# Store order, bias-gradient sums and square placement in a one-core training step of a gated FFT filter and a squared-ReLU MLP

## Chip, core and metric

The kernel runs on one core of one Trainium2 chip. The metric is the device time of the core in microseconds, the median over several executions. A profile is one further execution, recorded by the hardware profiler; its times are measured from the span's start.

## The reference

The program computes a forward pass and all gradients of it, in bfloat16, for a sequence of 2048 rows of 1024 columns and a hidden width of 3584:

```python
g = sigmoid((x * gate_w).sum(-1))            # one gate per row
a = irfft2(rfft2(x) * (w_r + 1j * w_i))      # spectral filter over both axes
h = relu(x @ w1 + b1) ** 2                   # MLP, squared relu
b = h @ w2 + b2
out = g * a + (1 - g) * b
# outputs: out, and the gradients of x, w_r, w_i, w1, b1, w2, b2, gate_w for a given grad_out
```

The gradient of b2 is the sum over the 2048 rows of `db = (1 - g) * grad_out`, one number for each of the 1024 columns.

## The kernel before

The kernel is written in a tile framework: the program text gives each instruction a priority, and a scheduler puts each engine's instructions into a fixed order when the kernel is built. An instruction whose inputs are early can be put far ahead of its place in the text. `after(ins, earlier)` makes `ins` wait for `earlier`; with `NoSync` it only fixes the order of two instructions on the same engine. `later["last"]` is the eviction (`dhT`) that was written last in the text. `ld` issues a DMA from SP, `st` from POOL (GpSimd).

The work runs in stages. The change touches the first one, `mlp_in`, beside which the side work (`first_stage_of_x`, `first_stage_of_grad`, `fft_mid`) is spread in small steps, one and a half (later 1.15) to each step of the main work.

**The first passes.** Four passes `k` over 512 rows each load rows of x (`xsrc`) and of grad_out (`dbn`), compute the gate, scale `dbn` by it (`gate`, L664), and turn both into columns on TensorE (`turn_x`, `turn_grad`, results `xT` and `dbT`). For the first two column pairs of W1, `forth` computes the hidden layer and `back_` the gradient `dh` (matmuls `pd`, L742, evicted on VectorE to `dhT`, L746). Each pass stores its four gated row tiles to `db_scr` (L1620, and L1631 for the last), one MB each, and adds them up in float32 (`sum_of_db`, L1590). After the passes, `column_sums` and `sums_out` (L972 to L984) reduce that accumulator over the partitions: a transpose on VectorE, a reduction, a small matmul with `sel`, a copy and a store.

**The units.** For the other columns of W1, a `Unit` (fp, sp) computes a 256 by 1024 block of the hidden layer from seven products in place of eight. The sums of quarters of x (`x_sums`, L817, four for each half of the rows) lie in the memory of `dbn`, which they may overwrite only once its rows have been stored to `db_scr`; the sums of quarters of W1 (`w_sums`, L831) lie in `Sw`, or for odd fp in the last rows of `dbn`. Each unit's products p1, p5, p6, p7, p4, p3, p2 (of the next unit) are interleaved with four `back_` of the unit before, and the unit yields four times. The accumulator X is copied by ScalarE (`cu`, `u2`, L845) before TensorE may add the next product to it. `rest` makes the relu: for one of the four blocks ScalarE reads PSUM (L856); for the other three VectorE first adds the copied part and the bias (L858), and ScalarE then makes one relu over both blocks of c = 0 (L862) and one over the third (L860). The squares (L727) follow directly, and the store of `h2T` follows p3. W1's next columns are loaded by SP at the beginning of a unit with sp = 0, into one of two buffers (L764).

**The spectral side work.** `first_stage_of_x` does, for each row tile i: load a source (L635), `folds` on VectorE and ScalarE (L258 to L271), `row_stage` (matmuls `pk`, L279), `first_columns` (matmuls `pu`, evictions `w`, `u`, a store to `z_scr` in three DMAs, L228). `fft_mid` begins with `edges`, which gathers from `z_scr` the values at three frequencies in twelve small DMAs of 2-byte elements (L338 to L340): eight of them 64 partitions by 16 elements, four of 64 elements. Then it loads its filters (`ab`, `wn`) and inputs (`z`).

Of the kernel before, what the change touches and what calls it, by code (L numbers as in the profile page):

```python
# [10 lines left out]
P = 128  # L11
# [128 lines left out]
def kernel(  # L140
# [179 lines left out]
    def fft_mid(filler):  # L320
# [7 lines left out]
        def edges():  # L328

            ed = fb.tile([P, NM, 2, 4], FDT, name="ed", tag="ed")  # L330
            low = fb.tile([P, NM, 4], FDT, name="low", tag="low")
            mid = fb.tile([P, 4], FDT, name="mid", tag="mid")
            nc.vector.memset(ed[lanes[1], 0], 0.0)
            col = z_scr[:].rearrange("c r x h t l -> r c h l x t")[:, :, 0, 0]
            for x in range(2):
                for t in range(2):
                    e = 2 * x + t
                    ld(out=ed[lanes[0], :, 0, e], in_=col[:, 0:NM, x, t])  # L338
                    ld(out=low[lanes[1], :, e], in_=col[:, NM:, 1 - x, t])
                    ld(out=mid[lanes[0], e : e + 1], in_=col[:, NM, 1 - x, t : t + 1])  # L340
            return ed, low, mid
# [324 lines left out]
    def first_stage_of_x():  # L666
        f, ft = {0: folds(f1, xs[0], later["last"])}, {}
        for i in range(NT + 1):
            if i + 3 < NT:
                xs[i + 3] = source(i + 3, x_perm, later["last"])  # L670
            if i < NT:
                ft[i] = row_stage(f1, f[i], kf[:], later["last"])
                yield
            if i > 0:
                first_columns(f1, cf, 0, i - 1, ft[i - 1], later["last"])
            if i + 1 < NT:
                f[i + 1] = folds(f1, xs[i + 1], later["last"])
            yield
# [23 lines left out]
    def mlp_in():  # L702
# [23 lines left out]
        def squared(rT, h2T):  # L726
            nc.scalar.activation(h2T, rT, ACT.Square)  # L727
# [106 lines left out]
        class Unit:  # L834
# [8 lines left out]
            def copied(self, tag):  # L843
                t_ = wb.tile([P, SW], FP32, name=tag, tag=tag, bufs=1)
                nc.scalar.copy(out=t_[:], in_=self.X[:])  # L845
                return t_

            def rest(self, c, j, acc, add=None):
# [4 lines left out]
                whole = self.rT[c]  # L853
                rT = rTs[self.fp, s, c] = whole[:, j, :]
                if add is None:
                    nc.scalar.activation(rT, acc[:], ACT.Relu, bias=bias)  # L856
                else:
                    STT(out=rT, in0=acc[:], scalar=bias, in1=add[:], op0=ALU.add, op1=ALU.add)  # L858
                    if c:
                        nc.scalar.activation(rT, rT, ACT.Relu)  # L860
                if (c, j) == (0, 1):
                    nc.scalar.activation(whole[:], whole[:], ACT.Relu)  # L862
                if (c, j) in ((0, 1), (1, 0)):
                    squared(whole[:], h2_of(self.fp, self.sp)[:, c])
# [26 lines left out]
            def p3(self):  # L891
                self.chain(self.V, S_[self.fp][4], x_quads(self.sp)[1][1], False)
                self.rest(0, 1, self.V, self.u2)
                store(h2T_scr, h2.pop((self.fp, self.sp)), self.fp, self.sp)

        later["x_sums"] = x_sums
        load_w1(0)
# [23 lines left out]
        for n, u in enumerate(units_):  # L921
# [3 lines left out]
            u.p1()  # L925
            back_(*waiting[0])
# [3 lines left out]
            u.p6()  # L930
            back_(*waiting[1])
            next(more_sums, None)
            if u.sp == 1 and u.fp < LAST:
                w_sums(u.fp + 1)
# [7 lines left out]
            if pr == 0 and u.sp == 0:  # L942
                later["blocks"] = later["last"]
                if 0 < fg < FG - 1:
                    load_w2(fg + 1, later["last"])
            u.p4()
# [7 lines left out]
        again(slice(8, NT))  # L954
        more = [(LAST, s, c) for c in range(2) for s in range(2)]
# [628 lines left out]
    acc = f1.tile([P, D], FP32, name="gb2", tag="gb2")  # L1584

    def sum_of_db(n):
        if n == 1:
            V(out=acc[:], in0=dbn[:, 0, :], in1=dbn[:, 1, :], op=ALU.add)
        elif n:
            V(out=acc[:], in0=acc[:], in1=dbn[:, n, :], op=ALU.add)  # L1590

    sums_of_x = None
    for k in range(NT // 4):
# [13 lines left out]
        sum_of_db(i), sum_of_db(i + 1)  # L1607
# [5 lines left out]
        sum_of_db(i + 2)  # L1613
# [3 lines left out]
        sum_of_db(i + 3)  # L1617
        next(units)
        if k:
            st(out=db_scr[:, i - 4 : i, :], in_=dbn[:, i - 4 : i, :])  # L1620
# [9 lines left out]
        if k == 3:  # L1630
            st(out=db_scr[:, i : NT, :], in_=dbn[:, i : NT, :])  # L1631
# [6 lines left out]
    sums_out(f1, fps, "ps2", column_sums(f1, acc, "tr_"), out_7)  # L1638
# [84 lines left out]
```

## Time and profile before

| | |
|---|---|
| Median of 3 runs | 1269.1 us (1268.01 to 1273.19) |
| The profiled execution's own time | 1265.81 us |
| Its span, first to last instruction | 1264.0 us |
| Mean granted TensorE clock | 0.996 of full speed |
| TensorE matmuls busy | 1213.3 us, 96% of the span |
| VectorE busy | 849.8 us, 67% |
| ScalarE busy | 553.2 us, 44% |
| GpSimd busy | 373.1 us, 30% |
| DMA moved | 242.75 MB, mean 192 GB/s |

In the profile's lines PE is TensorE, PEld its weight loads, DVE VectorE, ACT ScalarE, POOL GpSimd and SP SyncE; L12 is line 12 of the kernel. A row of instructions names the output and the inputs of an operation by the program's names. In a timeline the first number is the start in us, the second the duration, and a bracket at the end is the time that the engine was idle before, with what ended that wait. The waits are listed as: engine, line and output that waited, what it waited for, us in total, number of times, the longest. In the page's second part each digit is the busy share, in tenths, of one of forty equal slices of the span. A few per cent of the matmul records are missing in a trace.

### The profile page before, as it was taken

What the parts mean: (1) busy time and instruction counts of PE and PEld (TensorE: products, weight loads), DVE (VectorE), ACT (ScalarE), POOL (GpSimd) and SP (SyncE); (2) the same over time, 40 slices, a digit from 0 to 9 for tenths busy, and PEclk for the clock granted to TensorE, in tenths of its full rate; (3) what the DMA queues carried; (4) which work ended last, traced back from release to release, by engine and by line L of the source; (5) the groups of instructions that cost most, each with busy time, mean ns of one, the idle gap of its engine ahead of it and who ended that gap; (6) DMA issues with size and microseconds to landing.
All of it is one profiled execution on the core that took longest, in us unless ns stands there. A gap on an engine that the chain in (4) does not pass through costs nothing.

```text
span 1264.0 us, 18724 instructions
## 1 busy us (share of the span) xinstructions
PE 1213.3 (96%) x6527; PEld 587.9 (47%) x6648; DVE 849.8 (67%) x1940; ACT 553.2 (44%) x1006; POOL 373.1 (30%) x620
## 2 busy tenths in 40 slices
PE   7998999997999999999999999999999999999998
PEld 4554545543444444444444445555445444444443
DVE  3987668744788779677766552443876765896573
ACT  3566768863777753444445544555222210011110
POOL 0123424421333332323335545654122010000000
PEclk9999999999999999999999999999999999999999
DMA  9868465765465989889969969985799987666520
GB/s 290 288 179 182 135 203 175 189 167 151 155 184 166 229 245 188 175 192 223 248 164 284 195 155 250 218 224 166 182 242 210 212 190 190 180 185 184 169 85 34
DMA packets 329593, 242.75 MB, mean 192 GB/s; under 512 B 197868, under 2 KB 284042, under 8 KB 328730
## 3 DMA queue, kind: packets, MB, share of 16 engines
q1 hardware_dynamic: 297968, 146.43, 51.8%
q0 software_dynamic: 31328, 95.07, 23.5%
q8 instruction: 52, 0.85, 0.3%
q14 instruction: 43, 0.35, 0.1%
q10 hardware_dynamic: 202, 0.04, 0.0%
HBM read 111.43 MB, written 86.00 MB: 156 GB/s over the span
## 4 chain that ended last, share of the span: by engine, by line
PE 71%; DVE 15%; ACT 4%; DMA 4%; issue 4%; SPq 2%; POOL 0%; DVEq 0%; ACTq 0%
PE pw L1206 15%; PE acc L1289 13%; PE pd L742 8%; PE xX L1399 7%; PE pX L1078 6%; PE ph L841 5%; PE pV L1078 4%; PE xV L1399 3%; ACT x L419 2%; PE xZ L1399 2%; SPq L181 2%; DVE dhT L746 1%; PE pui L312 1%; DMA w1g<-in_B_w_dram 1%; PE pki L565 1%
## 5 line engine op out<-in xcount | busy, mean ns | idle before, releaser
L742 PE MATMUL pd<-dbT,w2T 128*128 128x512 bf16 x859 | 209.5, 383 | 10.0 <-DVE dhT L746 6.8
L742 PEld LDWEIGHTS <-w2T 128*128 128x128 bf16 x896 | 87.3, 99 | 111.3 <-issue 15.1
L1206 PEld LDWEIGHTS <-res 128*128 128x128 bf16 x896 | 86.6, 98 | 99.6
L1206 PE MATMUL pw<-odd,res 128*128 128x512 bf16 x498 | 112.5, 379 | 0.7
L746 DVE SCALAR_TENSOR_TENSOR dhT<-pd,rT 128x512 bf16<-128x512 f32 x112 | 76.7, 685 | 44.4 <-PE pd L742 38.3
L1357 ACT ACTIVATE g<-gatew_bc,dsc 128x1024 f32<-128x1024 bf16 x16 | 18.3, 1148 | 177.3 <-DVE dT L1408 98.3
L1206 PE MATMUL pw<-even,res 128*128 128x512 bf16 x374 | 84.0, 379 | 0.5
L419 ACT CAST x<-px 64x512 f16<-64x512 f32 x128 | 74.2, 579 | 19.7 <-PE px L416 18.4
L228 POOL DMA_DIRECT2D z_scr<-u x96 | 58.7, 617 | 80.8 <-ACT u L296 40.8
L228 POOL DMA_DIRECT2D r<-y_scr x96 | 58.5, 613 | 72.8 <-issue 41.5
L1399 PEld LDWEIGHTS <-dS 128*128 128x128 f16 x448 | 43.8, 98 | 53.3 <-DVE dS L1386 0.5
L1208 ACT CAST wo<-pw 128x512 bf16<-128x512 f32 x56 | 32.6, 584 | 81.8 <-PE pw L1206 81.8
L1289 PEld LDWEIGHTS <-even 128*128 128x128 bf16 x448 | 43.4, 98 | 50.3
L1289 PEld LDWEIGHTS <-odd 128*128 128x128 bf16 x448 | 43.2, 98 | 49.3
L1290 DVE SCALAR_TENSOR_TENSOR ot<-acc,omg,af 128x512 bf16<-128x512 f32 x32 | 24.0, 749 | 56.2 <-PE acc L1289 56.1
L727 ACT ACTIVATE h2T<-rT 128x1024 bf16<-128x1024 bf16 x56 | 59.1, 1057 | 0.7
L1289 PE MATMUL acc<-w2high,even 128*128 128x512 bf16 x249 | 57.1, 379 | 0.4
L1289 PE MATMUL acc<-w2high,odd 128*128 128x512 bf16 x249 | 57.0, 379 | 0.4
L1078 PEld LDWEIGHTS <-S 128*128 128x128 f16 x336 | 32.4, 98 | 45.6 <-DVE S L1065 7.4
L456 POOL DMA_DIRECT2D y_scr<-pc x64 | 36.1, 564 | 52.4 <-DVE pc L453 46.0
L1399 PE MATMUL xX<-dT,dS 128*128 128x512 f16 x224 | 51.0, 379 | 0.1
L394 POOL COPY w<-wn 128x512 bf16<-128x512 bf16 x32 | 23.8, 744 | 90.1 <-DVE tt L427 79.1
(262 smaller groups left out, 2496.1 us busy)
## 6 DMA issues: line engine op xcount, KB each, us to landing
h2T_scr<-h2T POOLq DMA_DIRECT2D x28, 512.0 KB, 4.4
dhT_scr<-dhT POOLq DMA_DIRECT2D x28, 512.0 KB, 4.8
z<-z_scr SPq DMA_DIRECT2D x64, 128.0 KB, 3.2
y_scr<-pc POOLq DMA_DIRECT2D x64, 128.0 KB, 4.1
ax_scr<-yo POOLq DMA_DIRECT2D x32, 256.0 KB, 4.5
out_dram<-wo POOLq DMA_DIRECT2D x56, 128.0 KB, 5.0
even<-h2T_scr SPq DMA_DIRECT2D x8, 896.0 KB, 8.7
odd<-h2T_scr SPq DMA_DIRECT2D x8, 896.0 KB, 7.3
```

Source lines behind the costliest of these rows:

```text
L228: issue(out=a, in_=b) if stored else issue(out=b, in_=a)
L419: nc.scalar.copy(out=x[lanes[n], c, :, 0:HW], in_=px[lanes[c], n])
L456: st(out=y_scr[:][c, :, :, h].rearrange("r x t l -> (r x) t l"), in_=pc[:, n])
L727: nc.scalar.activation(h2T, rT, ACT.Square)
L742: mm(pd[:], lhsT=w_[:, ec, fc % FGC * P : (fc % FGC + 1) * P], rhs=dbT[:, ec, ss], start=(ec == 0), stop=(ec == DC - 1),)
L746: return STT(out=dhT, in0=pd[:], scalar=2.0, in1=rT, op0=ALU.mult, op1=ALU.mult, accum_out=gb1part[:, fc, sb : sb + 1],)
L841: mm(acc[:], lhsT=lhs[:, t, :], rhs=rhs[:, t, :], start=start and t == 0, stop=t == KH - 1, skip_group_check=True)
L1078: self.mm = mm(acc[:], lhsT=lhs[:, t, c_], rhs=rhs[:, t, :], start=start and t == 0, stop=t == KH - 1, skip_group_check=True,)
L1206: mm(pw[:], lhsT=xr[:, t, d_ * P : (d_ + 1) * P], rhs=cur[:, t, :], start=(t == 0), stop=(t == NT - 1))
L1208: nc.scalar.copy(out=wo[:], in_=pw[:])
L1289: turn["PE"] = mm(acc[:], lhsT=cur[:, fc, t2 * P : (t2 + 1) * P], rhs=w2[fc // NT][:, fc % NT, cs], start=(fc == 0), stop=(fc == FC - 1))
L1399: mm(acc[:], lhsT=lhs[:, fc, :], rhs=rhs[:, fc, :], start=start and fc == 0, stop=fc == KH - 1, skip_group_check=True,)
```

## The change

Six edits, all in or beside the first stage:

1. The twelve edge loads of `edges` are issued by POOL (`st`) and not by SP (`ld`).
2. In `first_stage_of_x` the folds of tile i+1 are written ahead of the yield that separates `row_stage` of tile i from `first_columns` of tile i-1, and no longer behind `first_columns`.
3. In a `Unit`, both blocks of c = 0 get a relu of their own (512 columns each), and the squares leave `rest`: they are made in the next unit, the first ordered behind that unit's copy in p1, the second, followed by the store of `h2T`, behind its copy in p6.
4. The gradient of b2 is no longer accumulated from `dbn`. Sixteen reductions on VectorE sum halves of the rows of `dbT` (128 partitions by 1024 elements each), one in each of the units 1 to 16; in unit 17 the two halves are added, turned by one transpose on TensorE, copied and stored. They carry no order of their own.
5. `w_sums` moves from behind the second `back_` of a unit to behind the fourth and behind the sum of item 4.
6. The stores to `db_scr` wait for `later["last"]`. Pass 1 has none any more; pass 2 stores the rows of the first two passes, pass 3 those of the third, and the last follow as before. At these places `later["last"]` is the third eviction of pass 2's `back_`, and then the fourth.

```diff
@@ -335,9 +335,9 @@
             for x in range(2):
                 for t in range(2):
                     e = 2 * x + t
-                    ld(out=ed[lanes[0], :, 0, e], in_=col[:, 0:NM, x, t])
-                    ld(out=low[lanes[1], :, e], in_=col[:, NM:, 1 - x, t])
-                    ld(out=mid[lanes[0], e : e + 1], in_=col[:, NM, 1 - x, t : t + 1])
+                    st(out=ed[lanes[0], :, 0, e], in_=col[:, 0:NM, x, t])
+                    st(out=low[lanes[1], :, e], in_=col[:, NM:, 1 - x, t])
+                    st(out=mid[lanes[0], e : e + 1], in_=col[:, NM, 1 - x, t : t + 1])
             return ed, low, mid
 
         def some_am(h):
@@ -670,11 +670,11 @@
                 xs[i + 3] = source(i + 3, x_perm, later["last"])
             if i < NT:
                 ft[i] = row_stage(f1, f[i], kf[:], later["last"])
+                if i + 1 < NT:
+                    f[i + 1] = folds(f1, xs[i + 1], later["last"])
                 yield
             if i > 0:
                 first_columns(f1, cf, 0, i - 1, ft[i - 1], later["last"])
-            if i + 1 < NT:
-                f[i + 1] = folds(f1, xs[i + 1], later["last"])
             yield
 
     def first_stage_of_grad():
@@ -723,8 +723,8 @@
         def d_bank(name):
             return banks[-1].tile([P, SW], FP32, name=name, tag="ph", bufs=2)
 
-        def squared(rT, h2T):
-            nc.scalar.activation(h2T, rT, ACT.Square)
+        def squared(rT, h2T, behind_=None):
+            after(nc.scalar.activation(h2T, rT, ACT.Square), behind_, mybir.DependencyClass.NoSync)
 
         def new_rT():
             return wb.tile([P, 2, SW], BF16, name="rT", tag="rT", bufs=3)
@@ -842,7 +842,7 @@
 
             def copied(self, tag):
                 t_ = wb.tile([P, SW], FP32, name=tag, tag=tag, bufs=1)
-                nc.scalar.copy(out=t_[:], in_=self.X[:])
+                self.copy = nc.scalar.copy(out=t_[:], in_=self.X[:])
                 return t_
 
             def rest(self, c, j, acc, add=None):
@@ -850,18 +850,17 @@
                 bias = b1col[:, fc : fc + 1]
                 if c not in self.rT:
                     self.rT[c] = new_rT()
-                whole = self.rT[c]
-                rT = rTs[self.fp, s, c] = whole[:, j, :]
+                rT = rTs[self.fp, s, c] = self.rT[c][:, j, :]
                 if add is None:
                     nc.scalar.activation(rT, acc[:], ACT.Relu, bias=bias)
                 else:
                     STT(out=rT, in0=acc[:], scalar=bias, in1=add[:], op0=ALU.add, op1=ALU.add)
-                    if c:
-                        nc.scalar.activation(rT, rT, ACT.Relu)
-                if (c, j) == (0, 1):
-                    nc.scalar.activation(whole[:], whole[:], ACT.Relu)
-                if (c, j) in ((0, 1), (1, 0)):
-                    squared(whole[:], h2_of(self.fp, self.sp)[:, c])
+                    nc.scalar.activation(rT, rT, ACT.Relu)
+
+            def square(self, c, behind_=None):
+                squared(self.rT[c][:], h2_of(self.fp, self.sp)[:, c], behind_)
+                if c:
+                    store(h2T_scr, h2.pop((self.fp, self.sp)), self.fp, self.sp)
 
             def p2(self):
                 self.Z = d_bank("pZ")
@@ -891,9 +890,23 @@
             def p3(self):
                 self.chain(self.V, S_[self.fp][4], x_quads(self.sp)[1][1], False)
                 self.rest(0, 1, self.V, self.u2)
-                store(h2T_scr, h2.pop((self.fp, self.sp)), self.fp, self.sp)
 
         later["x_sums"] = x_sums
+        gb2 = wb.tile([P, DC, 2], FP32, name="gb2", tag="gb2")
+
+        def sum_of_db(n):
+            ec, h = divmod(n, 2)
+            nc.vector.reduce_sum(out=gb2[:, ec, h : h + 1], in_=dbT[:, ec, h * S // 2 : (h + 1) * S // 2], axis=mybir.AxisListType.X)
+
+        def grad_of_b2():
+            whole = wb.tile([P, DC], BF16, name="gb2b", tag="gb2b")
+            V(out=whole[:], in0=gb2[:, :, 0], in1=gb2[:, :, 1], op=ALU.add)
+            pb = fps.tile([DC, P], BF16, name="pb2", tag="ps2", bufs=2)
+            nc.tensor.transpose(pb[:], whole[:], identb[:])
+            row = wb.tile([DC, P], BF16, name="gb2r", tag="gb2r")
+            nc.vector.tensor_copy(out=row[:], in_=pb[:])
+            st(out=out_7.rearrange("(c p) -> c p", p=P), in_=row[:])
+
         load_w1(0)
         yield
         load_w1(1)
@@ -923,15 +936,17 @@
             if u.sp == 0 and u.fp < LAST:
                 load_w1(u.fp + 1)
             u.p1()
+            if n:
+                units_[n - 1].square(0, u.copy)
             back_(*waiting[0])
             u.p5()
             yield
             next(more_sums, None)
             u.p6()
+            if n:
+                units_[n - 1].square(1, u.copy)
             back_(*waiting[1])
             next(more_sums, None)
-            if u.sp == 1 and u.fp < LAST:
-                w_sums(u.fp + 1)
             yield
             u.p7()
             back_(*waiting[2])
@@ -943,6 +958,12 @@
                 later["blocks"] = later["last"]
                 if 0 < fg < FG - 1:
                     load_w2(fg + 1, later["last"])
+            if 0 < n <= 2 * DC:
+                sum_of_db(n - 1)
+            elif n == 2 * DC + 1:
+                grad_of_b2()
+            if u.sp == 1 and u.fp < LAST:
+                w_sums(u.fp + 1)
             u.p4()
             u.p3()
             if n + 1 < len(units_):
@@ -952,6 +973,7 @@
             if (u.fp, u.sp) == (LAST - 1, 0):
                 again(slice(0, 8))
         again(slice(8, NT))
+        units_[-1].square(0), units_[-1].square(1)
         more = [(LAST, s, c) for c in range(2) for s in range(2)]
         for this, that in zip(more, waiting):
             forth(*this, True)
@@ -1581,15 +1603,6 @@
     rows_of_x(1)
     st(out=cf[:], in_=cten["cf"].ap())
     stage = None
-    acc = f1.tile([P, D], FP32, name="gb2", tag="gb2")
-
-    def sum_of_db(n):
-        if n == 1:
-            V(out=acc[:], in0=dbn[:, 0, :], in1=dbn[:, 1, :], op=ALU.add)
-        elif n:
-            V(out=acc[:], in0=acc[:], in1=dbn[:, n, :], op=ALU.add)
-
-    sums_of_x = None
     for k in range(NT // 4):
         i = 4 * k
         if k + 1 < NT // 4:
@@ -1604,20 +1617,18 @@
         next(units)
         turn_grad(i + 3) if k else (turn_grad(i + 2), turn_grad(i + 3))
         next(units)
-        sum_of_db(i), sum_of_db(i + 1)
         if stage:
             next(stage)
         next(units)
         if k + 1 < NT // 4:
             turn_x(i + 4), turn_x(i + 5)
-        sum_of_db(i + 2)
         next(units)
         if k + 1 < NT // 4:
             turn_x(i + 6), turn_x(i + 7)
-        sum_of_db(i + 3)
         next(units)
-        if k:
-            st(out=db_scr[:, i - 4 : i, :], in_=dbn[:, i - 4 : i, :])
+        if k > 1:
+            for n in (i - 8, i - 4) if k == 2 else (i - 4,):
+                after(st(out=db_scr[:, n : n + 4, :], in_=dbn[:, n : n + 4, :]), later["last"])
         if k + 1 < NT // 4:
             gate(4 * (k + 1))
         if k + 2 < NT // 4:
@@ -1628,14 +1639,13 @@
             stage = first_stage_of_x()
         next(stage)
         if k == 3:
-            st(out=db_scr[:, i : NT, :], in_=dbn[:, i : NT, :])
+            after(st(out=db_scr[:, i:NT, :], in_=dbn[:, i:NT, :]), later["last"])
             for _ in later["x_sums"](0):
                 pass
         next(units)
         next(stage)
     V(out=gpg[:], in0=gcol[:], in1=omg[:], op=ALU.mult)
     later["more_banks"]()
-    sums_out(f1, fps, "ps2", column_sums(f1, acc, "tr_"), out_7)
 
     def aside():
         yield from stage
```

## The prediction

> **What bounds the kernel now.** I read the page first, then the table of windows of 20 us, then TensorE's waits, then the timeline around each long wait.
>
> ```profile
> PE   7998999997999999999999999999999999999998
> DVE  3987668744788779677766552443876765896573
> ACT  3566768863777753444445544555222210011110
> DMA  9868465765465989889969969985799987666520
> ```
>
> Each digit is 31.6 us. TensorE is full in the second half, so only its gaps can be won. The windows say where they lie: of 480 us up to 480, TensorE is idle for 33 us; from 560 to 1240 no window has over 0.9 us of it, except one of 1.6. The change touches only the first part. TensorE's waits from 87 to 470 us (total, times, longest):
>
> ```profile
> PE pd L742 <- DVE dhT L746: 6.6, 3, 5.9
> PE pk L279 <- ACT f L271: 6.4, 7, 2.8
> PE ph L841 <- ACT cu L845: 5.1, 6, 1.5
> ```
>
> One wait of 5.93 us is half of the first row and more. The timeline shows its chain (start, duration, engine, line; in brackets the idle time before it):
>
> ```profile
> 266.87 0.69 SPq L338 DMA_DIRECT2D ed<-z_scr  x1
> ...
> 277.54 0.92 SPq L340 DMA_DIRECT2D mid<-z_scr  x1
> ...
> 287.73 0.52 SPq L764 DMA_DIRECT2D w1g<-in_B_w_dram  x1
> ...
> 293.37 0.76 DVE L831 TENSOR_TENSOR dbn<-w1g 128x512 f16<-128x512 bf16 x2 [9.13 <-DMA w1g<-in_B_w_dram]
> 294.04 0.68 DVE L746 SCALAR_TENSOR_TENSOR dhT<-pd,rT 128x512 bf16<-128x512 f32 x1
> ...
> 294.79 4.93 PE L742 MATMUL pd<-dbT,w2T 128*128 128x512 bf16 x16 [5.93 <-DVE dhT L746]
> ```
>
> Twelve edge loads hold SP from 266.87 to 278.46. Behind them come filters and inputs, and the load of W1 only at 287.73. The sums of W1's quarters (L831) stand at the head of VectorE's queue for 9.13 us, the eviction dhT stands behind them, and TensorE stops. The 16 matmuls after it take 4.93 us where undisturbed rows of 16 take 3.45: the granted clock in the window 280 to 300 is 0.91. A smaller stretch of the same kind:
>
> ```profile
> 118.60 0.62 PE L279 MATMUL pk<-kf,f 128*128 128x128 f16 x8 [1.77 <-ACT f L271]
> ...
> 122.96 0.42 DVE L258 TENSOR_TENSOR uv<-src 128x512 f16<-128x512 bf16 x1 [3.32 <-DMA src<-in_A_x_dram]
> ...
> 126.23 0.62 PE L279 MATMUL pk<-kf,f 128*128 128x128 f16 x8 [2.82 <-ACT f L271]
> ```
>
> and the start of the kernel:
>
> ```profile
> 15.57 0.54 POOL L1620 DMA_DIRECT2D db_scr<-dbn  x1 [12.04 <-DVE dbn L664]
> ...
> 24.45 1.89 PE L642 MATMUL pt<-identb,xsrc 128*128 128x128 bf16 x16 [2.38 <-DMA xsrc<-in_A_x_dram]
> ...
> 31.31 1.23 DVE L817 TENSOR_TENSOR dbn<-xT 128x2048 f16<-128x2048 bf16 x1 [1.64 <-ACT xT L643]
> ```
>
> The last line matters for the order: L817 is written at the end of the fourth pass and runs at 31 us. What is not tied runs where its engine is free, far from where it is written.
>
> **The change, part by part.** Sums are against the profiled execution (span 1264.0, its own time 1265.8 us); the median of the three runs is 3.3 us above that.
>
> *Edge loads from SP to POOL, sums of W1 later.* SP loses 11.6 us of issuing. In the unit of 315 us, the W1 load is issued at 315.43, 0.03 us after the matmuls of p4 that free its buffer (314.37 plus 1.03). In the unit of 280 those matmuls end at 280.23 (279.20 plus 1.03), so the load could start 7.5 us before 287.73. The sums then start near 285.9, VectorE has waited 1.7 us instead of 9.13, and the wait of 5.93 and the slow matmuls' 1.48 go: -7.4 us. If ab, wn and z still keep SP, nothing is won: 0. I take -7.4, since these loads (278.50 to 287.63) need 9.1 us of SP and can begin at 267. W1's sums also move two turns back in the text; they ran before their place already, so I count nothing. POOL gets twelve issues. No row there has 1024 pieces of 2 bytes; 64 pieces take 0.54 us (gw), 256 take 0.73 (h2T), so I estimate 0.54 to 1.6 each, 6 to 15 us of POOL. Behind them on POOL stands dhT's store, at 267.44 now; its buffer is wanted again near 284, and a store lands 4.8 us after issue. Up to 12 us it costs nothing, at 15 it gives back 3.
>
> The Trainium skill, "DMA: Bandwidth & Descriptors", section "Issuing engines are not separate DMA queues", says that another issuing engine saves only the sequencer's time, usually small beside the transfer. Here the row shows 11.6 us of issue against 3.3 to 5.1 us of landing each; by that rule this part would be about 0, and the sum -1.6 instead of -9.0.
>
> *Stores of gated rows.* Now one MB each at 15.57, 35.03, 56.73 and 77.27. Tied behind the third and fourth evictions of the third pass (74.70 and 76.89), all four leave POOL between 75.4 and 79. Early, DMA is at 0.96 and 0.99 of its share; the wait of 2.38 us for xsrc, with a clock of 0.72 in the 5 us behind it (1.4 us), is worth up to 3.8 us. The load itself is issued late, behind SP's transposes (until 18.61), so I take -1.0. Later, three MB more meet a stretch at 1.0 (80 to 120). A store lands 5.0 to 10.1 us after issue, so the first two are down at 82 to 90. L817 overwrites those rows and must now wait; TensorE wants its result at 90.17, and on VectorE everything behind L817 waits too. Between 0 and +10 (8 of waiting and 1.5 of slow clock); I take +2.2, near the short end, since 65 to 75 has DMA idle at 0.01 to 0.26 and queues are short then.
>
> *Gradient of b2.* Removed: 15 adds of 1.21, the transpose of 1.23, the reduction of 1.21 and small pieces: 21 us of VectorE before 92, where DVE is the releaser of waits of 0.70 and 0.49 at 55 to 58 and in the chain of 1.21 at 60.63. L817 leaves that stretch too. Of these 2.4 I take -1.2, since early halves of the new sums can fill the holes. Added: 16 reductions of 128x1024, for which the nearest row is L975, 1.21: 19.4 us, and a last step of a few tenths. They are tied to nothing. VectorE is at 12 to 17 of 20 us from 120 to 260 and at 16 to 19 from 340 to 420. Bounds: 0 if all fill holes, +19.4 if each stands before an urgent eviction. VectorE waits 21 us for pd before its evictions between 80 and 300, so holes exist: I take an eighth, +2.4.
>
> *Folds a turn earlier.* VectorE and ScalarE get folds before first_columns, where both had stood 2 us behind z_scr stores (116.8). The wait of 1.77 at 118.60 should go, or most of it; the 2.82 at 126.23 hangs on src, issued at 115.06 behind SP's transposes, and stays. But uv then reaches the head of VectorE's queue a turn earlier and blocks evictions while src is missing: up to +4. From -6.3 (1.77, 2.82, and 1.7 of slow matmuls behind them: 1.77 us for four, 2.67 for eight, against 1.03 and 1.73) to +4; I take -1.5.
>
> *Squares behind copies.* Two squares of 1.06 leave the places ahead of the next unit's copies; the wide relu of 1.05 becomes two of 0.63, 0.2 us more per unit, hidden while ScalarE is at 6 to 17 of 20 (4.8 us over 23 units if it were not). TensorE's waits on cu and u sum to 5.6 us, all after 310 but the first, and L419's casts, which stay, stand in the same queue. Between -5.6 and +1; I take -2.5. The store of h2T comes half a unit later; its second buffer covers that (without it, a square would wait 4.4 us for the landing).
>
> Sum: -7.4 - 1.0 + 2.2 - 1.2 + 2.4 - 1.5 - 2.5 = -9.0, and 1269.1 - 9.0 = 1260 us.
>
> **Rivals.** (a) VectorE becomes the bound: the untied row sums, at 1.21 each, stand before evictions in units 1 to 16. For it: the wait at 284 shows that one held instruction there stops TensorE, and 340 to 420 has 1 to 4 us of holes in 20. Against: the 21 us of waiting for pd. If all of it counts, 19.4 - 2.4 more: 1277. It turns the sign once 0.7 us of each sum lies on the path (11.4 over 16). (b) The W1 load is not earlier, or POOL's edges hold dhT's store as long: without the 7.4, 1267.5, no change. For it: fourteen other loads stand between. (c) The four stores meet and L817 holds VectorE until 90: +8 on the forecast, 1268. Against: DMA is idle just before. (d) All the waits go, none comes: -7.4 - 3.8 - 2.4 - 6.3 - 5.6 is -26; half of what lies beyond my terms gives 1252.
>
> **How the numbers follow.** Forecast 0.44, (a) 0.20, (b) 0.16, (c) 0.10, (d) 0.10. A measurement of this kernel can tell 0.5% (6.3 us) from no change. Faster: (d) and most of the forecast, 0.52; same: (b), (c) and a little of the forecast, 0.28; slower: (a), 0.20. The range takes in (d) at its lower side with some more, and (a): 1249 to 1277. The faster cases alone run from 1249 to 1263.
>
> **What would show it.** Right: no VectorE wait above 3 us on w1g near 285, the clock at 1.00 in that window; the twelve ed, low, mid issues on POOL within 15 us; db_scr's four stores between 75 and 80; row sums in holes, with TensorE's waits on dhT under 2 us in all; waits on cu halved. Wrong: W1's load still issued over 5 us after p4, a VectorE wait on db_scr at L817, a new pk wait on src, or row sums in front of evictions from 100 to 360. A gain above 20 us or a loss would mean that the scheduler's order changed in ways that I don't see from here.

## The result and the profile after

The changed kernel takes 1254.84 us (median of 4 runs, 1248.74 to 1258.46) against 1269.13 before (4 runs, 1268.01 to 1273.19): a ratio of 0.9877, 95% interval 0.9831 to 0.9923. That is 14.3 us less; the forecast was 9.1 less. The profiled execution of after took 1253.29 us, its span is 1251.5 (12.5 less than before), and its mean granted clock is 0.997.

The page's second part, of after (each digit 31.3 us):

```profile
PE   8988999999999999999999999999999999999998
...
DVE  3869767746888868777866642444876765896573
ACT  4656867855777652444445544655222210011110
...
DMA  9587575786464979899979969995999787666530
```

Three of PE's digits moved: the first from 7 to 8, the third (63 to 94 us) from 9 to 8, and the tenth (284 to 316 us), which holds the W1 stall near 290 us, from 7 to 9; all others are the same. So this stall is gone, and something new stands in the third slice. The table of TensorE's waits from 87 to 470 us says what (total, times, longest):

```profile
PE ph L841 <- ACT u L845: 10.9, 6, 7.5
PE pu L312 <- ACT ft L283: 2.4, 3, 1.2
PE pk L279 <- ACT f L271: 2.0, 3, 0.8
...
PE pd L742 <- DVE dhT L746: 0.9, 2, 0.5
...
PE ph L841 <- ACT cu L845: 0.8, 2, 0.5
```

The dhT row fell from 6.6 to 0.9, pk from 6.4 to 2.0, cu from 5.1 to 0.8. In their place stands one row of 10.9 us for u, 7.5 of it in one wait, and a small one for ft. Without that one wait, u and cu together are 4.2 us, where before has 5.6.

The timeline round the W1 load, after (start, duration, engine, line; idle time before it in brackets):

```profile
264.19 0.84 POOL L338 DMA_DIRECT2D ed<-z_scr  x1
...
273.70 0.54 POOL L340 DMA_DIRECT2D mid<-z_scr  x1 [1.34 <-DMA ed<-z_scr]
...
274.99 0.73 POOL L773 DMA_DIRECT2D dhT_scr<-dhT  x1 [0.74 <-DMA low<-z_scr]
...
279.83 0.39 SPq L764 DMA_DIRECT2D w1g<-in_B_w_dram  x1
...
285.15 0.76 DVE L831 TENSOR_TENSOR dbn<-w1g 128x512 f16<-128x512 bf16 x2 [1.30 <-DMA w1g<-in_B_w_dram]
...
285.83 0.68 DVE L746 SCALAR_TENSOR_TENSOR dhT<-pd,rT 128x512 bf16<-128x512 f32 x1
```

The last `mid` and the first `dhT` store are POOL's now. SP issues the W1 load at 279.83 and no longer at 287.73. VectorE waits 1.30 us for it and not 9.13, dhT follows 0.68 us after the first pair of sums, and TensorE does not wait. In the window from 280 to 300 the clock is 1.00 (0.91 before).

The new wait, in the timeline round 95 us of after:

```profile
71.50 11.01 SPq L181 DMA_TRANSPOSE w2T<-in_B_w_dram  x2
...
82.57 2.44 SPq L635 DMA_DIRECT2D src<-in_A_x_dram  x2
...
85.11 8.17 SPq L764 DMA_DIRECT2D w1g<-in_B_w_dram  x2
...
93.37 9.85 SPq L635 DMA_DIRECT2D src<-in_A_x_dram  x2
95.41 0.42 DVE L258 TENSOR_TENSOR uv<-src 128x512 f16<-128x512 bf16 x1 [7.99 <-DMA src<-in_A_x_dram]
...
96.20 0.20 ACT L265 COPY f<-uv 128x2 f16<-128x2 f16 x1 [6.70 <-DVE uv L259]
96.30 0.58 ACT L845 COPY u<-ph 128x512 f32<-128x512 f32 x1
96.93 1.87 PE L841 MATMUL ph<-dbn,Sw 128*128 128x512 f16 x4 [7.49 <-ACT u L845]
```

It reads from the top. SP is held 11.01 us by the transposed loads of W2, then issues two sources (L635) from 82.57, then is held 8.17 by the loads of W1. The four stores of gated rows, four MB, were issued between 68 and 79. The DMA engines' share is 1.07 from 70 to 75 us and 1.08 from 75 to 80, where before has 0.26 and 0.55; from 80 to 100 it is 1.03, where before has 1.01 too. So from 80 us on they are about as full as in before; what differs is that they have been full for some ten us longer, with the stores and the transposes ahead of the sources. These are slow to land. From the list of DMA issues between 82 and 90 us of after (KB each, median us from issue to landing; the sources take 6.0 in before, where they are issued at 85.06, later than here):

```profile
w1g<-in_B_w_dram SPq DMA_DIRECT2D x2, 512.0 KB, 13.6
...
src<-in_A_x_dram SPq DMA_DIRECT2D x2, 256.0 KB, 12.8
```

The folds were moved a turn earlier, so `uv` is at the head of VectorE's queue and waits 7.99 us. ScalarE's small copy of `f` (L265) waits 6.70 for uv. Behind it in ScalarE's order stands the copy `u`, and TensorE waits 7.49 for that. From 96.9 to 101.0 the granted clock is 0.50, so those 4.1 us do the work of 2.05: the stall costs some 9.5 us in all. (The Trainium skill, "TensorE: Matmul & The Clock Gate", section "What's actually happening", says that a TensorE idle for a window of about 3.4 us falls to half its clock and comes back after about as long a busy stretch; the 0.50 over 4.1 us agrees. In before the clock is 0.72 from 25 to 30 us, behind a wait of 2.38 us, so a shorter one costs too.)

The four stores of gated rows and the sixteen row sums of after, from POOL's timeline and from the answer for one line:

```profile
68.53 1.39 POOL L1631 DMA_DIRECT2D db_scr<-dbn  x2 [3.97 <-DVE dhT L746]
...
75.66 0.58 POOL L1631 DMA_DIRECT2D db_scr<-dbn  x1
...
78.42 0.58 POOL L1642 DMA_DIRECT2D db_scr<-dbn  x1
```

```profile
L899 DVE TENSOR_REDUCE gb<-dbT x16: 1210/1214/1218, 39.0 to 133.3; 128x1 f32<-128x1024 bf16 x16
its engine sat idle before it (us, times) until:
who waited for it (us, times):
```

The stores leave POOL between 68.5 and 79; 75 to 80 was expected, and the third pass now ends some 6 us sooner. The sums ran from 39 to 133 us, VectorE was not held idle before any, and nobody waited for one. They are written in units 1 to 16, but are tied to nothing and took the first holes.

**One table for all kernels.** The 112 evictions `dhT` (L746) come in the same order of the text in every kernel. So the time between the starts of the 12th, 16th, 24th, 56th, 64th and 112th covers the same evictions, and the traces can be set side by side (us, one profiled execution each; the last column is what follows up to the end of the span). The side work beside it is spread alike: counted by the casts `ft`, as much of it lies before each mark in every kernel, but for one row tile that comes after the 24th eviction where the folds are late in the kernel after, and one that comes after the 16th in b_rowsums.

| kernel | to 12th | 12-16 | 16-24 | 24-56 | 56-64 | 64-112 | rest |
|---|---|---|---|---|---|---|---|
| before | 76.9 | 25.8 | 39.4 | 124.3 | 33.3 | 174.4 | 789.9 |
| after | 70.8 | 34.7 | 33.4 | 127.1 | 25.9 | 172.0 | 787.5 |
| before + edges (b_edges) | 78.4 | 25.8 | 41.3 | 124.5 | 26.1 | 174.2 | 787.5 |
| before + stores (b_stores) | 70.5 | 30.7 | 35.2 | 124.5 | 34.8 | 174.3 | 789.7 |
| before + squares (b_squares) | 76.0 | 25.8 | 34.9 | 127.3 | 31.9 | 171.6 | 788.8 |
| before + row sums (b_rowsums) | 75.7 | 33.4 | 41.5 | 124.5 | 34.5 | 174.6 | 790.3 |
| before + folds (b_folds) | 74.1 | 26.6 | 31.7 | 123.9 | 33.5 | 174.2 | 790.0 |
| before + sums of W1 (b_wsums) | 75.7 | 25.8 | 38.3 | 124.7 | 35.2 | 174.2 | 789.9 |
| after, edges back (a_edges_sp) | 70.3 | 36.7 | 33.4 | 127.1 | 32.3 | 171.6 | 788.8 |
| after, stores back (a_stores_early) | 75.2 | 31.9 | 31.2 | 126.7 | 29.8 | 172.2 | 787.5 |
| after, folds back (a_folds_late) | 71.3 | 28.2 | 32.9 | 129.5 | 26.6 | 172.2 | 787.4 |
| after, W2 early (a_w2_early) | 70.7 | 26.8 | 33.4 | 129.4 | 25.9 | 172.0 | 787.5 |

The kernels without an edit show how far a column moves by itself. Without the tied stores the first one runs from 74.1 to 78.4, with them from 70.3 to 71.3. 16-24 runs from 38.3 to 41.5 where stores, squares and folds are all as before. 24-56 is at most 124.7 without the new squares and at least 126.7 with them; 64-112 at least 174.2 and at most 172.2. 56-64 is 31.9 or more with the edges on SP, 29.8 or less with them on POOL. Before to after is -6.1, +8.9, -6.0, +2.8, -7.4, -2.4 and -2.4. Of the last, 1.3 lies behind the issue of the last store. It goes with the edges: that tail is 3.8 us in the five kernels of the table with the edge loads on POOL and 5.1 to 5.2 in the seven with them on SP. Why, no run shows.

The products of the units (L841) can run ahead of their place, so the columns 12-16 and 16-24 don't hold the same of them in every kernel. TensorE's busy time and the matmul records of L841 in both:

| kernel | 12-16: busy, L841 | 16-24: busy, L841 | 12-24 in all |
|---|---|---|---|
| before | 24.96, 22 | 33.91, 55 | 65.2 |
| b_stores | 28.23, 37 | 31.05, 43 | 65.9 |
| b_folds | 25.95, 30 | 30.72, 50 | 58.3 |
| b_squares | 24.96, 22 | 32.08, 54 | 60.7 |
| after | 26.82, 23 | 32.20, 56 | 68.1 |

For b_stores the two columns have to be read as one, since most of their +4.9 and -4.2 is work that changed its column; for b_folds about 1 us is. In after the longer busy time of 12-16 is the slow clock, not more work.

### The profile page after: what moved, and what is told of

Read it like the earlier page. It is cut to its first block, busy times and chain, and to the rows that moved or that the text cites. A ratio compares the mean times of both kernels' runs of the same rounds, so it can differ in the third digit from the quotient of the medians.

```text
span 1251.5 us, 18761 instructions
## 1 busy us (share of the span) xinstructions
PE 1209.6 (97%) x6525; PEld 588.6 (47%) x6647; DVE 845.5 (68%) x1940; ACT 555.1 (44%) x1029; POOL 381.2 (30%) x632
## 4 chain that ended last, share of the span: by engine, by line
PE 69%; DVE 13%; issue 6%; DMA 5%; ACT 4%; POOL 1%; SPq 1%; DVEq 0%; POOLq 0%; ACTq 0%
PE pw L1228 15%; PE acc L1311 15%; PE xX L1421 7%; PE pd L742 7%; PE pX L1100 5%; PE pV L1100 4%; PE ph L841 4%; PE xV L1421 3%; DMA w1g<-in_B_w_dram 2%; PE xZ L1421 2%; ACT x L419 2%; DVE dhT L746 1%; PE ph L735 1%; PE pui L312 1%; PE pki L565 1%
## 5 line engine op out<-in xcount | busy, mean ns | idle before, releaser
L746 DVE SCALAR_TENSOR_TENSOR dhT<-pd,rT 128x512 bf16<-128x512 f32 x112 | 76.7, 685 | 30.4 <-PE pd L742 28.1
L419 ACT CAST x<-px 64x512 f16<-64x512 f32 x128 | 74.1, 579 | 16.7 <-PE px L416 15.5
L858 ACT ACTIVATE rT<-rT 128x512 bf16<-128x512 bf16 x69 | 43.4, 629 | 51.2 <-DVE rT L857 51.0
```

Source lines behind the costliest of these rows:

```text
L419: nc.scalar.copy(out=x[lanes[n], c, :, 0:HW], in_=px[lanes[c], n])
L746: return STT(out=dhT, in0=pd[:], scalar=2.0, in1=rT, op0=ALU.mult, op1=ALU.mult, accum_out=gb1part[:, fc, sb : sb + 1],)
```

## The experiments

Each ratio is to the kernel before, with the 95% interval; the medians of before on the same chip were 1265.92, 1267.94 and 1265.94 us for the three groups of four below.

**b_edges: the edge loads alone.** The kernel before with the three lines `ld(out=ed ...)`, `low`, `mid` turned to `st`.

> The kernel before with only the twelve edge loads moved from SP to POOL; the order on VectorE is the same as before. Theory 1 (the late load of W1 was the cause of the 5.93 us wait): W1's load is issued within 1 us after p4, near 280; VectorE waits under 2 us for it; the window 280 to 300 has a clock of 1.00; the time falls by 6 to 8 us (ratio 0.994 to 0.995). Rival (the wait of that unit would have come from another load, or POOL's twelve issues hold the store of dhT): the wait changes its name and the time stays within 2 us of before.

Measured: 1257.47 us, 0.9924 (0.9898 to 0.9950). The load of W1 is issued at 283.85, 0.03 us after the matmuls of p4 that free its buffer (282.79 plus 1.03; all of it is later than 280 because the main work stands 3.6 us later here at the 56th eviction). VectorE waits 3.25 us for it, TensorE does not; the clock from 280 to 300 us is 1.00, and 56-64 takes 26.1 us in place of 33.3. The order on VectorE is that of before, so the load alone does it.

**a_edges_sp: all but the edge loads.** The kernel after with those three lines back on `ld`.

> The changed kernel with the twelve edge loads back on SP. Theory 1 (each part acts for itself): the W1 load is late by 5 to 8 us again, a wait of VectorE of over 6 us near 290 and of TensorE of 4 to 6 us are back, 6 to 8 us slower than the changed kernel, near 1262. Rival (the later place of W1's sums and the other order had already taken that wait away): the time is within 2 us of the changed kernel.

Measured: 1261.35 us, 0.9965 (0.9943 to 0.9988). The wait is back, as the timeline shows:

```profile
286.41 1.35 SPq L764 DMA_DIRECT2D w1g<-in_B_w_dram  x1
...
293.09 0.76 DVE L831 TENSOR_TENSOR dbn<-w1g 128x512 f16<-128x512 bf16 x2 [7.69 <-DMA w1g<-in_B_w_dram]
...
294.51 5.30 PE L742 MATMUL pd<-dbT,w2T 128*128 128x512 bf16 x16 [4.53 <-DVE dhT L746]
```

The load is issued at 286.41, VectorE waits 7.69, TensorE 4.53, and the 16 matmuls take 5.30 us. The column 56-64 is 6.4 us above after.

**b_stores: the tied stores alone.** The kernel before with item 6 of the change:

```diff
-        if k:
-            st(out=db_scr[:, i - 4 : i, :], in_=dbn[:, i - 4 : i, :])
+        if k > 1:
+            for n in (i - 8, i - 4) if k == 2 else (i - 4,):
+                after(st(...), later["last"])
```

> The kernel before with only the stores to db_scr tied and bunched. Theory 1 (four MB of stores meet the loads of 75 to 100 us and delay them): a wait of VectorE on src or on the stores of 3 to 8 us between 80 and 100, the time 2 to 9 us longer, less 1 to 3 us won at 24 us. Rival (the 7.5 us wait at 89 us in the changed kernel comes from its other order, not from the stores): no wait over 3 us there, the time 1 to 3 us shorter than before.

Measured: 1261.22 us, 0.9955 (0.9935 to 0.9976): a gain, where my two terms summed to a loss of 1.2. To the 12th eviction it is 6.4 us shorter: TensorE's waits for xsrc there fall from 4.5 us to 1.2, those for dhT from 1.4 to none, and the clock from 20 to 40 us rises from 0.91 to 1.00. From the 12th to the 24th it takes 65.9 us in place of 65.2, so almost nothing is given back. L817 does not wait for a store in this trace, and in no trace here over 1.2 us. The loads do land later. The DMA share is 1.04 and 1.10 in the two stretches from 70 to 80 us (0.26 and 0.55 in before), and in SP's timeline of this kernel

```profile
71.27 8.08 SPq L181 DMA_TRANSPOSE w2T<-in_B_w_dram  x2
79.40 4.37 SPq L635 DMA_DIRECT2D src<-in_A_x_dram  x2
83.88 8.51 SPq L764 DMA_DIRECT2D w1g<-in_B_w_dram  x2
92.48 6.97 SPq L635 DMA_DIRECT2D src<-in_A_x_dram  x2
```

transposes and W1 loads hold it for 8.08 and 8.51 us, where the same two take 6.27 and 1.29 in b_folds, which has the old stores. By the list of DMA issues its sources of this stretch land after 15.9 us (6.0 in before). But the folds are late here: `uv` needs the source at 94.6 and runs at 95.34 after a wait of 0.7 us, where in after it runs at 95.41 after a wait of 7.99. So neither wait that theory 1 named came, and the first half of the rival's forecast held: the late sources alone stop nobody.

**a_stores_early: all but the stores.** The kernel after with the stores of before.

> The changed kernel with the stores to db_scr as they were before (one after each pass, untied). Theory 1 (bunched stores delay the source load that VectorE waits 7.99 us for): that wait falls below 2 us, the clock in 80 to 100 is 1.00, the wait of 2.4 us on xsrc near 24 us is back; in sum 4 to 8 us faster than the changed kernel, near 1248. Rival (the loads of 71 to 95 us, two transposes, two of W1 and four sources, are late by themselves): the wait stays within 2 us of 8, the time is that of the changed kernel or 2 us more.

Measured: 1252.22 us, 0.9891 (0.9868 to 0.9915), not to be told from after. The table has both halves: the first passes lose 4.4 us, 12-16 wins 2.8 and 16-24 another 2.2, 56-64 loses 3.9. The wait of uv is gone (the source lands in 6.8 us), but VectorE waits 5.35 us for W1 up to 91.66, and TensorE 5.11 behind that. In 56-64 VectorE waits 5.2 us for W1 and TensorE 2.0 for dhT; why that load is later than in after, no run shows.

**a_folds_late: all but the folds.** The kernel after with the folds behind `first_columns` again.

> The changed kernel with the folds back behind first_columns. Theory F (folds a turn earlier put VectorE's wait for the source of a tile, 7.99 us at 87 to 95, ahead of the copy that TensorE needs, and so make the wait of 7.49 us): that wait falls to 3 us or less, waits on pk of 0.7 to 3 us between 95 and 130 are back, 3 to 8 us faster than the changed kernel. Rival (the source is late by the DMA alone and whatever needs it stops everything): the wait stays at 6 to 9 us, and with the pk waits the time is 0 to 4 us more.

Measured: 1249.89 us, 0.9856 (0.9830 to 0.9882). The 7.49 wait is gone, though the source still takes 10.2 us to land, and 12-16 takes 28.2 us in place of 34.7. From the 16th to the 56th it is 1.9 longer than after. In the profiles the early folds cost more than they bring, by 3.4 us, and by the ratios 2.7; but the intervals of the two ratios overlap widely (after: 0.9831 to 0.9923), so the times alone don't show that the early folds cost anything in this kernel. What is shown is that the stall goes with them.

**a_w2_early: the source ahead of the transposes.** The kernel after, with the second group of W2 loaded a pass earlier, so that SP is through with it when the sources are due:

```diff
             if s == 1:
                 load_w1(2)
-            if s == 2:
                 load_w2(1, later["last"])
```

> The changed kernel with the second group of W2's transposing loads (SP, 71.5 to 82.5 us) asked for one pass earlier, at the end of the second pass, when both its buffers are free and DMA is at 0.47 of its share (40 to 60 us). Theory S (what makes the source late at 95 us is SP's queue: two transposes of 11 us, then two loads of W1, ahead of it): the transposes are issued near 50, VectorE's wait on the source falls from 8.0 to under 2 us, the clock in 80 to 100 goes from 0.86 to 1.00, and the kernel is 6 to 10 us faster than the changed one, near 1246. Rival (the four bunched stores keep the DMA queues full whatever SP issues): the wait stays above 5 us and the gain is under 3 us.

Measured: 1246.65 us (1246.02 to 1251.18), 0.9840 (0.9815 to 0.9864). SP's timeline:

```profile
52.68 10.86 SPq L181 DMA_TRANSPOSE w2T<-in_B_w_dram  x2
68.15 4.80 SPq L635 DMA_DIRECT2D src<-in_A_x_dram  x3
75.26 4.73 SPq L764 DMA_DIRECT2D w1g<-in_B_w_dram  x2
88.05 7.38 SPq L635 DMA_DIRECT2D src<-in_A_x_dram  x2
```

The transposes are at 52.68, the sources follow at 68.15 (those issued from 64 to 100 us land in 3.5 to 6.5 us), and uv does not wait. The four stores leave where they left in after (68.42 to 78.31). 12-16 takes 26.8 us with the early folds and the tied stores both in place; 2.3 come back in 24-56, 1.7 of them in TensorE's busy time, at a clock of 0.94 from 230 to 260 us; I have no cause for it. So this stall needs all three: folds early, stores late, and the transposes beside the stores.

**b_squares: the squares alone.** The kernel before with item 3.

> The kernel before with only the squares, the relus and the store of h2T moved. By the sum: waits on cu fall from 5.1 to 2.5 us or less, the time is 2 to 3 us shorter. Rival (the copies are held by L419's casts and not by squares, or u2 now waits in place of cu): TensorE's waits on cu and u together stay at 5 to 6 us and the time within 1.5 us of before.

Measured: 1257.52 us, 0.9922 (0.9895 to 0.9948), far more than the 2.5 us of my term. TensorE's waits from 300 to 480 us, before and then in this kernel:

```profile
PE ph L841 <- ACT cu L845: 4.9, 5, 1.5
...
PE ph L841 <- ACT u L845: 0.5, 1, 0.5
```

```profile
PE ph L841 <- ACT u L845: 2.7, 4, 1.2
...
PE ph L841 <- ACT cu L845: 0.8, 2, 0.5
```

The copy cu gets its place, but u now waits: 5.4 us became 3.5. 64-112 shortens by 2.8. In 24-56 it loses 3.0, of which 2.4 are waits of TensorE for the casts `ft` (L283), before which squares now stand. What I had not counted is 16-24, shorter by 4.5 us: the pk waits from 60 to 140 us are 3.0 in all, not 6.8 (4.6 to 8.4 in the kernels whose stores, squares and folds are those of before).

**b_rowsums: the gradient of b2 alone.** The kernel before with item 4.

> The kernel before with only the gradient of b2 by row sums; the sums of W1 stay where they were. By the sum: +1.2 (-1.2 of early waits, +2.4 of evictions held up in the units). Rival 1 (VectorE becomes the bound): up to 17 us slower, with TensorE waiting for dhT over 10 us in all. Rival 2 (the sixteen sums run ahead of their place into VectorE's holes before 130 us): 1 to 4 us faster, waits on dhT as before.

Measured: 1271.40 us, 1.0030 (1.0010 to 1.0049), between my +1.2 and rival (a)'s +17, close to the first. No row sum has a waiter in the trace. In its profile, at 1276.35 us the longest of its runs, one long wait has no like in before:

```profile
92.77 0.76 DVE L831 TENSOR_TENSOR dbn<-w1g 128x512 f16<-128x512 bf16 x2 [6.60 <-DMA w1g<-in_B_w_dram]
...
98.70 3.57 PE L742 MATMUL pd<-dbT,w2T 128*128 128x512 bf16 x8 [6.24 <-DVE rT L858]
```

With the adds gone from VectorE, the sums of W1's quarters get to the head of its queue at 86 us, before W1 is there, and TensorE stands for 6.24. a_stores_early, the other kernel with row sums and the old stores, has the same wait for W1 there (5.35).

**b_folds: the folds alone.** The kernel before with item 2.

> The kernel before with item 2 alone: the folds of tile i+1 are written ahead of the yield. By the sum in the prediction, -1.5 us (pk waits get shorter by about 1.8, nothing new). Theory F, from the revert of this item in the kernel after (median 5 us below the kernel after): the uv sums reach the head of VectorE's queue before their source has landed and hold what stands behind them; then +2 to +5 us here, and the profile shows a VectorE wait of over 4 us for src between 60 and 130 us, with a wait of TensorE for u, f or dhT behind it. Rival: the folds hurt only together with the bunched stores, which meet the source loads; then 0 +- 1.5 here and no src wait longer than the 3.3 us that the kernel before has.

Measured: 1255.58 us, 0.9921 (0.9896 to 0.9945). Both expectations missed it, since it gains 10 us; of the rival's, only that no long wait on src comes held. TensorE's waits from 60 to 140 us, before and then here:

```profile
PE pk L279 <- ACT f L271: 6.8, 5, 2.8
```

```profile
PE pk L279 <- ACT f L271: 0.4, 1, 0.4
...
PE ph L841 <- ACT u L845: 0.3, 1, 0.3
```

All but 0.4 us of the pk waits go, and no long one comes. The wait of 2.82 at 126.23, which the prediction took to stay because its source stands behind SP's transposes, goes too: these hold SP for 6.82 us from 101.40 here, and for 11.18 from 103.43 in before, and no uv waits. 16-24 falls from 39.4 to 31.7 us: 7.7, or 6.9 for 12-24 as a whole, somewhat more than the 6.3 that I had named as the best end. Its list of DMA issues from 78 to 90 us says why uv blocks nothing:

```profile
src<-in_A_x_dram SPq DMA_DIRECT2D x2, 256.0 KB, 6.6
```

A source lands in 6.6 us here, not in 12.8. What hurts the early folds is the slow source, and without the bunched stores the source is in time.

**b_wsums: the sums of W1 alone.** The kernel before with item 5.

> The kernel before with item 5 alone: the sums of W1's quarters are written two turns later. By the prediction nothing: they ran ahead of their place already, so VectorE still has them at the head of its queue near 284 us, waits about 9 us for w1g and TensorE loses about 5.9 us; the time within 1.5 us of the kernel before. Rival: the place counts; dhT evictions that stood behind the sums now stand ahead of them, VectorE's wait at 290 shrinks below 6 us and TensorE's below 3, and the time falls by 2 to 5 us.

Measured: 1267.31 us, 1.0005 (0.9986 to 1.0025). Nothing; VectorE still waits 9.7 us for W1, TensorE 6.5.

**a_w2_early_folds_late and a_stores_each_w2: what is left.** The first is a_w2_early with the folds back. The second is a_w2_early with one MB stored after each pass, still tied:

```diff
-        if k > 1:
-            for n in (i - 8, i - 4) if k == 2 else (i - 4,):
-                after(st(out=db_scr[:, n : n + 4, :], ...), later["last"])
+        if k:
+            after(st(out=db_scr[:, i - 4 : i, :], ...), later["last"])
```

> The kernel after with two edits: the transposed loads of the second group of W2 one pass earlier (as in a_w2_early), and the folds back behind first_columns (as in a_folds_late). Theory S: both edits cure the same thing, the uv sum that waits for a source queued behind the transposes; then together they give what the better gives alone, 1246.7 +- 2, and not the sum of both (about 1242). Rival: they act on different waits (folds early also blocks VectorE elsewhere); then 1240 to 1244. Second rival: with the sources early, early folds are of use (they take pk waits away), and undoing them costs 2 to 4: 1249 to 1251.

> The kernel after with two edits: the transposed loads of W2 one pass earlier, and the stores of gated rows tied but one MB after each pass (passes 1, 2 and 3, then the last) in place of two MB after pass 2. If the bunching of four MB between 68 and 79 us still costs something after the W2 loads have moved, 2 to 4 us below a_w2_early: 1242 to 1245. If the stores cost nothing there, the same: 1246.7 +- 2. If a store during the early passes again delays xsrc (a wait near 23 us, as in a_stores_early), 1248 to 1251.

Measured: 1247.10 us, 0.9856 (0.9831 to 0.9880), and 1245.44 us, 0.9849 (0.9821 to 0.9877). Neither differs from a_w2_early. Two cures together give what one gives, as they would for one stall; 12-16 is 27.0 and 27.5, and the source lands in 4.8 and 3.6 us. In a_stores_each_w2 the first store leaves at 49.82 and the 12th eviction still comes at 70.5. So the gain of the first passes comes from the stores having left their early places (15, 35 and 57 us), not from their being bunched. Of the versions run, the three with W2 early are the fastest. Their medians are 8 to 9 us below after; by the ratios to before it is 3 to 5 us, and the intervals overlap with that of after.

## Why the prediction was right, and where it was not

The range from 1249 to 1277 holds 1254.84, and faster was the likeliest. The time lies between the forecast and rival (d), all waits gone, somewhat nearer to (d) at 1252; but (d) did not happen, since a new wait came. The sum was right in fewer terms than its total suggests. Each edit alone, its ratio times 1269.1 us, beside my term:

| item | term | alone | in the table, where it acts |
|---|---|---|---|
| edges on POOL | -7.4 | -9.6 | 56-64: -7.2 |
| stores tied | -1.0 + 2.2 | -5.7 | to 12th: -6.4; 12-24: +0.7 |
| gradient of b2 | -1.2 + 2.4 | +3.8 | 12-16: +7.6; 16-24: +2.1 |
| folds earlier | -1.5 | -10.0 | 12-24: -6.9 |
| squares | -2.5 | -9.9 | 16-24: -4.5; 24-56: +3.0; 64-112: -2.8 |
| sums of W1 | 0 | +0.6 | none |
| sum | -9.0 | -30.8 | measured together: -15.6 |

**Edges: right in size and by its steps.** The load was to start 7.5 us sooner and started 7.9 sooner; sums at 285.9 (285.15), a wait of 1.7 (1.30). The twelve issues took 8.8 us of POOL (eight of 0.82 to 0.84, four of 0.54), inside 6 to 15. dhT's store behind them left at 274.99 and held nobody. Rival (b) fell. Moving the issues was worth 9.6 us by the ratio (interval 6.3 to 12.9); in the profile 56-64 is 7.2 shorter and the last column 2.4, and the other columns, which vary as much by themselves, are 3.4 longer in sum. What counted was that one load on the path stood behind them on SP. The Trainium skill, "DMA: Bandwidth & Descriptors", section "Issuing engines are not separate DMA queues", calls the sequencer's time usually small beside the transfer; by that this part was to be about 0, and in this kernel it was not.

**Stores: wrong in sign, and in place.** I sized the early gain at 1.0 by one wait for xsrc; to the 12th eviction it is 6.4. I had seen that wait, its slow clock and DMA at 0.96 and 0.99, and argued the price down because SP issues that load late. The step that failed is this discount, and the count: it was the longest of three waits for xsrc, 4.5 us in all, of which 1.2 stay. For the price later I looked at L817, which waits for the landing of the stores. It waited 1.2 us at most, so rival (c) fell. The loads beside the stores paid: sources that land in 10 to 16 us and not in 6, W1's and W2's loads that hold SP. Alone that costs TensorE little (0.7 us in 12-24); in the change, where the folds need the source a turn earlier, it makes the stall.

**Folds: both ends of the range were real, in different kernels.** -6.3 to +4 was written down with the mechanism of each: pk waits that go, and uv at the head of the queue before its source. Alone the first holds in full (-7.7 in 16-24, -6.9 in 12-24) and the second not at all. In the change the second holds at twice its size (7.49 of waiting and 2.05 of slow clock, of the +8.9 in 12-16). My -1.5 was a mean of two cases. What decided was whether another edit makes the source late, and I had costed the edits one by one.

**Squares: the mechanism right, the size off.** I took 2.5 from the cu and u waits after 310 us, and 64-112 gave 2.8. Two stretches were missing, both where ScalarE also runs the folds. In 16-24 the kernel won 4.5, and in 24-56 it lost 3.0, since squares now stand ahead of the casts `ft`. I had looked at what the squares leave, not at what stands behind them in their new places. That it is the squares' old places ahead of the copies of `f` that made the pk waits in 16-24 is my reading of these rows; it was not tried by itself.

**Gradient of b2: right in kind.** The row sums went into holes, and rival (a), VectorE as the bound, which had 0.20, was not seen. The +3.8 comes from another side: sums of W1 pulled ahead and waiting for their load. That this is the whole of it is read from one trace and was not tried.

**Why the sum was near all the same.** The single gains add to 30.8 us, the change brings 15.6. In 16-24 folds and squares take 7.7 and 4.5 us from the same waits for f: 12.2 one by one, while the whole change takes 6.0. The stretch has not much more to give: TensorE is busy for 33.9 of its 39.4 us in before, and 31.2 is the least of any kernel. And in 12-16 stores, folds and row sums meet. My undersized gains and the overlap that I did not count cancelled in part. That the total came near is in good part luck: of the six terms only that of the edges, and the nothing for the sums of W1, were right in size.

What I listed to look for came out as follows: no wait above 3 us on w1g near 285, clock 1.00 there, POOL's issues within 15 us, sums in holes, dhT under 2 us, cu more than halved; the four stores came from 68.5 on and not from 75. Of the list of wrong signs, one came: a new wait on src, with u as the one who pays, not pk.

## What to carry to other kernels

When several edits aim at waits in the same stretch, set an upper limit for the stretch (its idle time and slow clock) before summing, and cost each edit once more with the others in place. A step moved earlier on an in-order engine needs its input's transfer to be earlier too: read the issuing engine's queue back from that transfer, and ask what else will be in flight. Bulk stores that nobody needs soon are best kept out of the stretch in which loads are on the path; then see which loads they meet in the new one.

## What the runs showed that I had not expected

- With four MB of stores just ahead, SP's own issues take longer: two W1 issues held SP 1.29 us in b_folds, 8.51 in b_stores and 8.17 in after, and a pair of transposes 6.27, 8.08 and 11.01. In a_folds_late, with the same stores, the two W1 issues come later, at 89.4, and take 1.76. The DMA share doesn't tell these apart (from 80 to 90 us 1.11 and 1.10 in b_folds, 1.40 and 0.82 in after).
- Twelve gathers of 2-byte elements take 8.8 us of issuing on POOL and held SP for 11.6; on POOL the larger ones land in 7.3 and 7.8 us (median), on SP in 3.6 and 5.1.
- A stall costs more than its length: TensorE's wait of 7.49 us was followed by 4.1 us at a granted clock of 0.50 (2.05 us more).
